# A new order of loads at the start of an attention and maxout kernel

## The chip, the cores and the metric

The kernel runs on one core of a Trainium2 chip. The core has TensorE (PE, matrix products into the accumulators called PSUM), VectorE (DVE), ScalarE (ACT), GpSimd (POOL) and SyncE (SP, which here only issues transfers), and sixteen DMA engines that all queues share. The metric is the device time of one execution in microseconds: the median of three runs.

## The reference, cut to what matters

Attention with a soft cap over 8 batches of 12 heads, 448 positions of 64 numbers, followed by a layer that takes the larger of two products:

```python
# q, k, v: (8, 12, 448, 64) f32, cap = 30
scores = cap * tanh((q @ k^T) / sqrt(64) / cap)
attn = exp(scores - max(scores)); attn = attn / (sum(attn) + 1e-9)
x = (attn @ v), heads side by side: (3584, 768)

h1 = x @ w1            # w1, w2: (768, 1024)
h2 = x @ w2
g = maximum(h1, h2)
out = g @ w_out        # w_out: (1024, 768), out: (3584, 768) f32
```

The kernel uses max(h1, h2) = h2 + relu(h1 - h2), so that

```
out = relu(x @ (w1 - w2)) @ w_out + x @ (w2 @ w_out)
```

It therefore prepares two matrices of its own: `wd_sb` = w1 - w2 (subtractions) and `wm_sb` = w2 @ w_out (transpositions of w2 and products on TensorE). After that each batch costs three products, with `wd_sb`, `wm_sb` and w_out.

## The kernel before

Two heads make a pair, two pairs a quad; there are 48 pairs and 24 quads. Three pairs make a group, and q, k, v are loaded group by group as f32, then cast to bf16. Groups 0 and 1 are transposed on TensorE (`transposes(i)`, one pair each); groups 2 and up by a transfer that transposes (`cross(g)`). Quad 0 needs pairs 0 and 1 (group 0), quad 1 pairs 2 (group 0) and 3 (group 1), quad 2 pairs 4 and 5 (group 1), quad 3 pairs 6 and 7 (group 2).

The loads and the preparation of the two matrices:

```python
    def load_wo(f):            # two of the eight 128-row pieces of w_out, 0.79 MB, cast on the way
        nc.gpsimd.dma_start(
            out=wo_sb[:, f : f + 2, :], in_=moe_w_out[f * P : (f + 2) * P, :].rearrange("(c p) n -> p c n", p=P)
        )

    def load_w2(c):            # one of the six 128-row pieces of w2, 0.52 MB, cast on the way
        nc.gpsimd.dma_start(out=w2b[:, c, :], in_=x_rows(moe_w2, c))

    def load_w1(c):
        w1_in[c] = opool.tile([P, DF], f32, name="osb") if c < OB else w1x[:, (c - OB) * DF : (c - OB + 1) * DF]
        nc.sync.dma_start(out=w1_in[c], in_=x_rows(moe_w1, c))

    def subtract(c, eng=nc.vector):
        eng.tensor_sub(wd_sb[:, c, :], w1_in[c], w2b[:, c, :])

    def turn_w2(c):            # 8 transpositions on TensorE, then one copy
        ps = mm_psum.tile([P, 512], f32, name="mm").bitcast(bf16)
        for f in range(FC):
            nc.tensor.transpose(ps[:, f * P : (f + 1) * P], w2b[:, c, f * P : (f + 1) * P], ident)
            yield
        w2T[c] = stage.tile([P, FC * P], bf16, name="w2T", bufs=2)
        nc.vector.tensor_copy(w2T[c], ps)

    def premultiply(c):        # 2 x 8 products
        for half in range(2):
            # ... ps = w2T[c] @ wo_sb[half], one product per yield ...
            nc.vector.tensor_copy(wm_sb[:, c, hs], ps[:, : DM // 2])
```

`w2b` lies in the buffer that later holds `gT`, the relu of the first product, so the first relu has to wait until w2 has been used up.

Scores go in three steps of two products into PSUM, each followed by tanh on ScalarE; `ex` is the exponential. `s_psum` has two buffers, `v_psum` one, and `mm_psum` two:

```python
    def scores(t, p, last=None):
        tanh[t, p] = att.tile([P, 2 * NJ, S], bf16, name="tanh")
        for j in range(NJ if p < 2 else 1):
            s = two_banks(last if last and j == NJ - 1 else s_psum)
            # ... two products into s ...
            nc.scalar.activation(tanh[t, p][:, 2 * j : 2 * j + 2, :], s[:, :, :S], AF.Tanh, scale=scale / cap)
```

`total(t)` sums the exponentials of a quad, `values(t)` multiplies them with v, `normalize` divides. All other TensorE work waits in a queue, and `F(n)` takes n products or transpositions from it, between the steps of the attention:

```python
    def F(n):
        rate[1] += n * rate[0]
        while rate[1] >= 1 and fill_q:
            try:
                next(fill_q[0])
                rate[1] -= 1
            except StopIteration:
                fill_q.pop(0)
```

The order in front, before the change (each engine works in this order):

```python
    fill_const(nc.vector, 0)
    load(0, "k", 0, 1); load(0, "q", 0, 1); load(0, "k", 1, L); load(0, "q", 1, L)
    load(1, "k"); load(1, "q"); load(0, "v")
    # ... casts of group 0's first pair ...
    for c in range(2): load_w2(c)
    for f in range(0, FC, 2): load_wo(f)
    fill_const(nc.gpsimd, 1)
    # ... transposes(0..2), scores and ex of quad 0, turn_w2(0) ...
    cast(nc.gpsimd, 1, "k"); cast(nc.gpsimd, 1, "q")
    for c in range(2, KC): load_w2(c)
    cast(nc.gpsimd, 0, "v", halves=(1,))
    load(1, "v"); load(2, "k"); load(2, "q")
    for c in range(KC): load_w1(c)
    # ... turn_w2(1); quad 1 with premultiply_first(0..8) and transposes(3..5) between ...
    cross(2)
    load(3, "k"); load(3, "q"); load(2, "v")
    # ... the queue gets turn_w2(2..5) and premultiply(1..5) ...
    total(0); scores(2, 0); ex(2, 0)
    F(4)
    normalize(0, values(0))
    F(8)

    for t in range(1, NQ):
        if t > 1:
            F(24 if t == 2 else 0)
            if more: scores(t + 1, 0, v_psum)
            ex(t, 2)
            F(6)
        if t == 2:
            # casts of k, q of group 3, cross(3), subtract(4), subtract(5) on POOL
        # ... F(2) F(3) F(3) F(2) with the sums of the exponentials between, if t > 1 ...
        if more: scores(t + 1, 1, v_psum)
        # ... F(3) F(4) F(3) F(4) ...
        if t == 1:
            for c in range(4): subtract(c, nc.gpsimd)
        F(8)
        if more: scores(t + 1, 2); ex(t + 1, 1)
        total(t)
        normalize(t, values(t))
        if t % 3 == 2: fill_q.append(moe(t // 3))   # 48 + 84 or 112 products of one batch
        F(9)
    F(10 ** 9)
```

Of the kernel before, what the change touches and what calls it, by code (L numbers as in the profile page):

```python
# [10 lines left out]
def kernel(  # L11
# [11 lines left out]
    nc = tc.nc  # L23
# [9 lines left out]
    P = 128  # L33
# [75 lines left out]
    def raw_of(g, what):  # L109
        if (g, what) not in raw:  # L110
            if (g, what) == (1, "v"):
                raw["unused"] = raw_tile(what)
            raw[g, what] = raw_tile(what)
        t = raw[g, what]
        m = t[:, : 2 * L * NJ * D].rearrange("p (h c) -> p h c", c=NJ * D)
        l = t[:, 2 * L * NJ * D :].rearrange("p (h d) -> p h d", d=D)
        return t, m, l
# [28 lines left out]
    def cast(eng, g, what, n0=0, n1=L, halves=(0, 1)):  # L146
# [52 lines left out]
    w1_in = {}  # L199
    w2b = (  # L200
        xpool.tile([P, FC, 2 * S], bf16, name="gT", bufs=1)
        .rearrange("p f s -> p (f s)")[:, : KC * DF]
        .rearrange("p (c n) -> p c n", c=KC)
    )

# [9 lines left out]
    def load_w2(c):  # L215
        nc.gpsimd.dma_start(out=w2b[:, c, :], in_=x_rows(moe_w2, c))

    w1x = xpool.tile([P, NP, 2 * S], bf16, name="xT").rearrange("p c s -> p (c s)").bitcast(f32)

    def load_w1(c):  # L220
        w1_in[c] = opool.tile([P, DF], f32, name="osb") if c < OB else w1x[:, (c - OB) * DF : (c - OB + 1) * DF]
        nc.sync.dma_start(out=w1_in[c], in_=x_rows(moe_w1, c))

    def subtract(c, eng=nc.vector):
        eng.tensor_sub(wd_sb[:, c, :], w1_in[c], w2b[:, c, :])

    w2T = {}

    def turn_w2(c):
        ps = mm_psum.tile([P, 512], f32, name="mm").bitcast(bf16)  # L230
        for f in range(FC):
            nc.tensor.transpose(ps[:, f * P : (f + 1) * P], w2b[:, c, f * P : (f + 1) * P], ident)
            yield
        w2T[c] = stage.tile([P, FC * P], bf16, name="w2T", bufs=2)
        nc.vector.tensor_copy(w2T[c], ps)

    def premultiply(c):

        for half in range(2):
            hs = slice(half * (DM // 2), (half + 1) * (DM // 2))  # L240
            ps = mm_psum.tile([P, 512], f32, name="mm")
            for f in range(FC):
                nc.tensor.matmul(  # L243
                    ps[:, : DM // 2], w2T[c][:, f * P : (f + 1) * P], wo_sb[:, f, hs],
                    start=(f == 0), stop=(f == FC - 1),
                )
                yield
            nc.vector.tensor_copy(wm_sb[:, c, hs], ps[:, : DM // 2])

# [37 lines left out]

    def scores(t, p, last=None):

        tanh[t, p] = att.tile([P, 2 * NJ, S], bf16, name="tanh")  # L290
        for j in range(NJ if p < 2 else 1):
            s = two_banks(last if last and j == NJ - 1 else s_psum)
# [98 lines left out]
    def moe(b):  # L391
        if b % 2 == 0:
            gT[b // 2] = xpool.tile([P, FC, 2 * S], bf16, name="gT", bufs=1)
        g, x = gT[b // 2], xT[b // 2]
        cs = slice((b % 2) * S, (b % 2 + 1) * S)
        for f in range(FC):
            ps = mm_psum.tile([P, 512], f32, name="mm")
            for c in range(KC):
                nc.tensor.matmul(  # L399
                    ps[:, :S], wd_sb[:, c, f * P : (f + 1) * P], x[:, c, cs], start=(c == 0), stop=(c == KC - 1)  # L400
                )
                yield
            nc.vector.tensor_relu(g[:, f, cs], ps[:, :S])  # L403
        for t in range(3) if b % 2 == 0 else range(3, 7):
            osb = opool.tile([P, DF], f32, name="osb")[:, :DM]
            ts = slice(t * P, (t + 1) * P)
            for half in range(2):
# [5 lines left out]
                for f in range(FC):  # L413
                    nc.tensor.matmul(  # L414
                        ps[:, : DM // 2], g[:, f, ts], wo_sb[:, f, hs], start=False, stop=(f == FC - 1)
                    )
                    yield
# [54 lines left out]

    fill_const(nc.vector, 0)
    load(0, "k", 0, 1)
    load(0, "q", 0, 1)
    load(0, "k", 1, L)
    load(0, "q", 1, L)
    load(1, "k")
    load(1, "q")
    load(0, "v")  # L480
    cast(nc.vector, 0, "k", 0, 1)
    cast(nc.gpsimd, 0, "q", 0, 1)
    for c in range(2):
        load_w2(c)
    for f in range(0, FC, 2):
        load_wo(f)
    fill_const(nc.gpsimd, 1)
    transposes(0)
    cast(nc.vector, 0, "k", 1, L)
    cast(nc.vector, 0, "q", 1, L)  # L490
    scores(0, 0, v_psum)
    ex(0, 0)
    transposes(1)
    scores(0, 1, v_psum)
    ex(0, 1)
    transposes(2)
    for _ in turn_w2(0):
        pass
    scores(0, 2)
    ex(0, 2)  # L500
    cast(nc.gpsimd, 1, "k")
    cast(nc.gpsimd, 1, "q")
    for c in range(2, KC):
        load_w2(c)
    cast(nc.gpsimd, 0, "v", halves=(1,))
    load(1, "v")
    load(2, "k")
    load(2, "q")
    for c in range(KC):
        load_w1(c)  # L510

    first = {}
# [23 lines left out]

    for _ in turn_w2(1):
        pass
    scores(1, 0, v_psum)
    transposes(3)  # L540
    cast(nc.vector, 0, "v", halves=(0,))
    cast(nc.gpsimd, 1, "v")
    cast(nc.gpsimd, 2, "k")
    cast(nc.gpsimd, 2, "q")
    ex(1, 0)
    premultiply_first(0, 2)
    scores(1, 1)
    ex(1, 1)
    premultiply_first(2, 4)
    transposes(4)  # L550
    premultiply_first(4, 6)
    scores(1, 2)
    ex(1, 2)
    transposes(5)
    cross(2)
    load(3, "k")
    load(3, "q")
    load(2, "v")
    premultiply_first(6, 8)
    for c in range(1, KC):  # L560
        if c + 1 < KC:
            fill_q.append(turn_w2(c + 1))
        fill_q.append(premultiply(c))
    total(0)
    scores(2, 0)
    ex(2, 0)
    F(4)
    normalize(0, values(0))
    F(8)

    for t in range(1, NQ):
        i = 2 * t
        more = t + 1 < NQ
        if t > 1:
            F(24 if t == 2 else 0)
            if more:
                scores(t + 1, 0, v_psum)
            ex(t, 2)
            F(6)
        if t in crosses:  # L580
            cross(crosses[t])
        if t == 2:
            cast(nc.gpsimd, 3, "k")
            cast(nc.gpsimd, 3, "q")
            cross(3)
            for c in range(4, KC):
                subtract(c, nc.gpsimd)
        if t == 3:
            cast(nc.gpsimd, 3, "v")
        if t > 2:  # L590
            extra(i)
        if t > 1:
            F(2)
            add(t, 0, 0)
            F(3)
            add(t, 0, 1)
            F(3)
            add(t, 1, 0)
            F(2)
        if more:  # L600
            scores(t + 1, 1, v_psum)
            ex(t + 1, 0) if t > 1 else None
        F(3)
        add(t, 1, 1)
        F(4)
        if t == 2:
            cast(nc.gpsimd, 2, "v")
            load(3, "v")
        F(3)
        add(t, 0, 2)  # L610
        F(4)
        add(t, 1, 2)
        if t == 1:
            for c in range(4):
                subtract(c, nc.gpsimd)
        if t == 2:
            extra(4)
            extra(5)
        if t > 2:
            extra(i + 1)  # L620
# [47 lines left out]
```

## Time and profile before

| | |
|---|---|
| time, median of 3 runs | 347.79 us (347.23 to 348.45) |
| span of the profiled execution | 345.9 us |
| TensorE busy | 326.2 us (94%) |
| ScalarE busy | 277.2 us (80%) |
| VectorE busy | 227.4 us (66%) |
| GpSimd busy | 109.8 us (32%) |
| moved by DMA | 61.78 MB |
| group 1's k and q, issued by 3.7 us | cast from 10.8 and 15.2 us on |
| crossbar transpose of group 2 | issued at 38.2 us, used at 48.3 us |

A busy share is taken over the whole span, which has stages with different limits; the start is a stage of its own. The profile counts a transfer's bytes as written: the loads of w2 and w_out, which cast from f32 to bf16 on the way, read twice what it shows. "Software queue" is the queue of the transfers that GpSimd issues, "hardware queue" that of SyncE.

### The profile page before, as it was taken

The page shows a single profiled execution, that of the slowest core. Times are in us where ns is not written, and L with a number is a line of the kernel's source. Part 1 is how long each engine was busy: PE and PEld are TensorE (multiplying, and loading weights), DVE is VectorE, ACT ScalarE, POOL GpSimd, SP SyncE. Part 2 cuts the span into 40 slices and gives each one's busy share as a digit, 9 for nine tenths or more (in the row PEclk, how much of TensorE's full clock was granted, in tenths as well). Part 3 has the DMA queues.
Part 4 walks back from the last instruction along what each step waited for, and adds up shares of the span by engine and source line. Part 5 has one row for each costly group of instructions (what it writes and reads, how often), then busy time and mean ns, then how long its engine had stood idle before and what let it go on. Part 6 is the DMA issues. An engine that isn't in the chain of part 4 may idle for free.

```text
span 345.9 us, 6777 instructions
## 1 busy us (share of the span) xinstructions
PE 326.2 (94%) x2710; PEld 163.3 (47%) x2710; DVE 227.4 (66%) x410; ACT 277.2 (80%) x241; POOL 109.8 (32%) x172
## 2 busy tenths in 40 slices
PE   3669979999999999999999999999999999999996
PEld 1324545445544554455444454454445554555563
DVE  5324645886777767777687768767776777874421
ACT  3998939989999999899999999799989999900000
POOL 6653848542144134304413431341343040000000
PEclk9959999999999999999999999999999999999999
DMA  7999999997695969775985499839956921012032
GB/s 253 252 253 242 369 204 180 247 213 199 132 295 158 211 149 282 205 172 123 252 252 100 134 230 300 179 96 216 307 124 143 209 96 46 2 47 91 0 93 91
DMA packets 103200, 61.78 MB, mean 179 GB/s; under 512 B 62337, under 2 KB 98177, under 8 KB 103169
## 3 DMA queue, kind: packets, MB, share of 16 engines
q1 hardware_dynamic: 101216, 58.21, 65.1%
q0 software_dynamic: 1952, 3.15, 5.0%
q8 instruction: 21, 0.34, 0.4%
q14 instruction: 11, 0.08, 0.1%
HBM read 42.47 MB, written 11.01 MB: 155 GB/s over the span
## 4 chain that ended last, share of the span: by engine, by line
PE 80%; DMA 13%; DVE 5%; issue 1%; SPq 0%; DVEq 0%
PE mm L414 22%; PE mm L399 19%; PE mm L411 16%; DMA kr<-in_k_dram 9%; PE v L366 6%; PE s L303 6%; DMA qkT<-kqf 3%; PE v L303 2%; PE s L300 2%; PE v L372 2%; PE mm L243 2%; PE s L350 2%; DMA osb<-in_moe_w_dram 1%; DVE xT L387 1%; DVE gT L403 1%; DVE st L352 1%
## 5 line engine op out<-in xcount | busy, mean ns | idle before, releaser
L309 ACT ACTIVATE expo<-tanh 128x2688 bf16<-128x2688 bf16 (+1 forms) x72 | 140.3, 1950 | 0.8 <-PE v L366 0.6
L304 ACT ACTIVATE tanh<-s 128x896 bf16<-128x896 f32 x122 | 106.4, 914 | 24.3 <-PE s L303 20.2
L414 PE MATMUL mm<-wo_sb,gT 128*128 128x384 bf16 x448 | 85.8, 327 | 0.0
L399 PE MATMUL mm<-xT,wd_sb 128*128 128x448 bf16 x384 | 78.8, 353 | 1.9 <-DVE gT L403 1.4
L411 PE MATMUL mm<-wm_sb,xT 128*128 128x384 bf16 x336 | 66.0, 326 | 0.4 <-DVE gT L403 0.4
L414 PEld LDWEIGHTS <-gT 128*128 128x128 bf16 x448 | 42.3, 98 | 34.7 <-issue 8.5
L418 DVE COPY osb<-mm 128x384 f32<-128x384 f32 x56 | 31.1, 555 | 40.7 <-PE mm L414 40.3
L399 PEld LDWEIGHTS <-wd_sb 128*128 128x128 bf16 x384 | 35.8, 98 | 41.2 <-issue 11.0
L403 DVE TENSOR_SCALAR gT<-mm 128x448 bf16<-128x448 f32 x64 | 39.4, 622 | 17.7 <-PE mm L399 17.2
L628 POOL COPY mark<-inv 1x1 f32<-1x1 f32 x18 | 3.2, 177 | 141.0 <-DVE inv L356 125.7
L411 PEld LDWEIGHTS <-xT 128*128 128x128 bf16 x336 | 31.7, 98 | 25.9 <-issue 5.9
L304 ACT ACTIVATE tanh<-v 128x896 bf16<-128x896 f32 x46 | 42.5, 923 | 0.0
L366 PE MATMUL v<-expo,vp 128*32 128x448 bf16 x576 | 35.6, 353 | 0.0
L303 PE MATMUL s<-qkT 64*128 64x448 bf16 x196 | 29.1, 371 | 6.7 <-ACT tanh L304 3.1
L387 DVE TENSOR_TENSOR xT<-v,inv 128x448 bf16<-128x448 f32 x48 | 27.8, 620 | 4.4 <-PE v L372 2.0
L352 DVE STREAM_TRANSPOSE st<-s 128x448 f32<-128x448 f32 x24 | 15.6, 650 | 19.8 <-PE s L350 17.5
L329 DVE TENSOR_TENSOR esum<-expo 128x896 bf16<-128x896 bf16 x42 | 27.9, 665 | 0.0
L327 DVE TENSOR_TENSOR esum<-esum,expo 64x896 bf16<-64x896 bf16 x42 | 26.6, 633 | 1.3
L331 DVE TENSOR_TENSOR esum<-esum,expo 128x896 bf16<-128x896 bf16 x42 | 26.7, 637 | 1.0
L303 PEld LDWEIGHTS <-qkT 64*128 64x128 bf16 x288 | 10.6, 96 | 29.7 <-issue 21.3
L366 PEld LDWEIGHTS <-vp 128*32 128x32 bf16 x576 | 15.3, 97 | 10.0
L183 POOL CAST kqf<-kr 128x1152 bf16<-128x1152 f32 x14 | 15.9, 1137 | 10.5 <-DMA kr<-in_k_dram 10.3
(66 smaller groups left out, 257.1 us busy)
## 6 DMA issues: line engine op xcount, KB each, us to landing
kr<-in_k_dram SPq DMA_DIRECT2D x14, 576.0 KB, 7.2
qr<-in_q_dram SPq DMA_DIRECT2D x14, 576.0 KB, 7.0
vr<-in_v_dram SPq DMA_DIRECT2D x14, 576.0 KB, 4.9
out_dram<-osb SPq DMA_DIRECT2D x20, 384.0 KB, 3.5
out_dram<-osb SPq DMA_DIRECT2D x16, 192.0 KB, 3.3
osb<-in_moe_w_dram SPq DMA_DIRECT2D x4, 512.0 KB, 8.6
gT<-in_moe_w_dram POOLq DMA_DIRECT2D x6, 256.0 KB, 12.8
wo_sb<-in_moe_w_out_dram POOLq DMA_DIRECT2D x4, 384.0 KB, 16.0
```

The lines of the kernel that those rows point to most:

```text
L303: nc.tensor.matmul(s[:, m, :S], k0[r, j * P : (j + 1) * P], qTn[r, :])
L304: nc.scalar.activation(tanh[t, p][:, 2 * j : 2 * j + 2, :], s[:, :, :S], AF.Tanh, scale=scale / cap)
L309: nc.scalar.activation(expo[t, p], tanh[t, p][:, 0:n, :], AF.Exp, scale=float(cap))
L329: nc.vector.tensor_add(d, e_of(t, ab, 0), e_of(t, ab, 1))
L331: nc.vector.tensor_add(d, d, e_of(t, ab, 2))
L366: nc.tensor.matmul(ps[r, :S], vp[g % 2][:, 2 * n + h, j, u::2], e_of(t, ab, j)[:, h, :], start=(j == 0), stop=False,)
L387: nc.vector.tensor_mul(x_of(t, u), ps[:, u, :S], inv[t])
L399: nc.tensor.matmul(ps[:, :S], wd_sb[:, c, f * P : (f + 1) * P], x[:, c, cs], start=(c == 0), stop=(c == KC - 1))
L403: nc.vector.tensor_relu(g[:, f, cs], ps[:, :S])
L411: nc.tensor.matmul(ps[:, : DM // 2], x[:, c, ts], wm_sb[:, c, hs], start=(c == 0), stop=False)
L414: nc.tensor.matmul(ps[:, : DM // 2], g[:, f, ts], wo_sb[:, f, hs], start=False, stop=(f == FC - 1))
L418: nc.vector.tensor_copy(osb[:, hs], ps[:, : DM // 2])
```

## The change

The order of the loads in front changes. The first piece of w2 and all of w_out now come directly behind group 0's q and k. Group 1's q, k, v are held back: a transfer of a single element of w_out into group 1's k buffer is put into the software queue in the middle of w_out, and since the load of k writes the same place, it has to wait for it. All loads of SyncE behind it wait with it. Group 1 is loaded and cast pair by pair, with pieces of w2 between. The products w2 w_out of the first piece are made between the scores of quads 0 and 1, as the pieces of w_out come; the rest is taken from the queue from quad 1 on. w1 is loaded in two column halves behind the transpose of group 2, w2 and `gT` lie in two half buffers, and subtractions are made by halves, partly on VectorE. The purpose is that TensorE has products to make while it would wait in front, and that what it needs first is loaded first.

The core of the diff:

```diff
-            if (g, what) == (1, "v"):
-                raw["unused"] = raw_tile(what)
...
     def load_w2(c):
-        nc.gpsimd.dma_start(out=w2b[:, c, :], in_=x_rows(moe_w2, c))
+        for part in range(2):
+            nc.gpsimd.dma_start(out=w2b[part][:, c, :], in_=x_rows(moe_w2, c)[:, part * DH : (part + 1) * DH])
...
-    def load_w1(c):
+    def load_w1(c, part):
...
-    def scores(t, p, last=None):
+    def scores(t, p, last=None, js=None):
...
-    for _ in turn_w2(1):
+    def load_and_cast(g, n):
+        for what in ("k", "q"):
+            load(g, what, n, n + 1)
+        for what in ("k", "q"):
+            cast(nc.gpsimd, g, what, n, n + 1)
+
+    fill_q.append(turn_w2(1))
+    fill_q.append(premultiply(1, 0))
+    for c in range(2, KC):
+        fill_q.append(turn_w2(c))
+        fill_q.append(premultiply(c - 1, 1))
+        fill_q.append(premultiply(c, 0))
+    fill_q.append(premultiply(KC - 1, 1))
+
+    fill_const(nc.vector, 0)
+    fill_const(nc.gpsimd, 1)
+    for n0, n1 in ((0, 1), (1, L)):
+        for what in ("k", "q"):
+            load(0, what, n0, n1)
+    load_w2(0)
+    load_wo(0)
+    load_wo(2)
+    nc.gpsimd.dma_start(out=raw_of(1, "k")[0][:1, :1], in_=moe_w_out[:1, :1])
+    load_wo(4)
+    load_wo(6)
+    load_w2(1)
...
+    scores(0, 0, v_psum)
+    ex(0, 0)
+    transposes(1)
+    scores(0, 1, js=(0, 1))
+    transposes(2)
+    for _ in turn_w2(0):
         pass
+    premultiply_first(0, 2)
+    scores(0, 1, js=(2,))
+    ex(0, 1)
+    scores(0, 2)
+    ex(0, 2)
+    load_and_cast(1, 0)
+    load_w2(2)
+    load_and_cast(1, 1)
+    load_w2(3)
+    load(0, "v")
+    cast(nc.gpsimd, 0, "v", halves=(1,))
+    load_and_cast(1, 2)
+    for c in range(4, KC):
+        load_w2(c)
+    load(2, "k")
+    load(2, "q")
+    load(1, "v")
     cast(nc.gpsimd, 2, "k")
     cast(nc.gpsimd, 2, "q")
+    cast(nc.gpsimd, 1, "v", halves=(1,))
+    premultiply_first(2, 4)
+    scores(1, 0, js=(0,))
+    premultiply_first(4, 6)
+    scores(1, 0, js=(1,))
+    premultiply_first(6, 8)
+    scores(1, 0, js=(2,))
     ex(1, 0)
+    transposes(3)
+    F(8)
+    scores(1, 1, v_psum)
     ex(1, 1)
+    F(24)
     transposes(4)
     scores(1, 2)
     ex(1, 2)
     cross(2)
     load(3, "k")
     load(3, "q")
+    for c in range(KC):
+        load_w1(c, 0)
+    cast(nc.vector, 0, "v", halves=(0,))
     total(0)
+    normalize(0, values(0))
     scores(2, 0)
     ex(2, 0)
+    F(14)
+    transposes(5)
+    scores(2, 1, v_psum)
+    F(6)
+    cast(nc.vector, 1, "v", halves=(0,))
+    F(6)
+    scores(2, 2)
+    ex(2, 1)
+    total(1)
+    normalize(1, values(1))
+    F(9)
+
+    for t in range(2, NQ):
...                       # pass t == 2:
+            for c in range(KC):
+                load_w1(c, 1)
+            load(2, "v")
+            load(3, "v")
+            for part in range(2):
+                for c in range(4 - part):
+                    subtract(c, part, nc.gpsimd)
...
+            for c in range(4, KC):
+                subtract(c, 0, nc.vector)
...                       # pass t == 3:
+            for c in range(3, KC):
+                subtract(c, 1, nc.vector)
```

## The prediction

> **What bounds the kernel now.** I read first the page's busy shares and its forty slices, then the busy time by stage of the first 60 us, then what TensorE (PE) waited for, and last the timeline around 38 to 60 us. The page:
>
> ```profile
> PE 326.2 (94%) x2710; PEld 163.3 (47%) x2710; DVE 227.4 (66%) x410; ACT 277.2 (80%) x241; POOL 109.8 (32%) x172
> ...
> PE   3669979999999999999999999999999999999996
> ...
> ACT  3998939989999999899999999799989999900000
> ...
> PEclk9959999999999999999999999999999999999999
> ```
>
> PE is full from the seventh slice (about 52 us) to the end, and ScalarE (ACT) has nothing more to do in the last five. So everything after about 60 us is PE's work in one unbroken stream, and the end comes earlier only if that stream starts earlier or has less in it. The change takes no matrix multiplication away; it can win only where PE stands idle or runs at half clock, in the first 50 us. By stage (columns: window, length, busy of PE, PEld, DVE, ACT, POOL, granted clock, DMA share, GB/s):
>
> ```profile
> 5.00:10.00 5.00, 3.09 (x46) 1.50 (x42) 2.95 (x6) 3.09 (x4) 4.92 (x10) 1.00 1.04 343
> ...
> 15.00:20.00 5.00, 2.46 (x37) 1.15 (x35) 1.02 (x2) 4.97 (x5) 3.44 (x6) 0.73 1.11 268
> 20.00:25.00 5.00, 2.97 (x11) 0.92 (x11) 2.04 (x4) 4.97 (x6) 2.20 (x4) 0.50 1.13 249
> 25.00:30.00 5.00, 5.00 (x76) 2.73 (x77) 1.41 (x3) 4.74 (x5) 2.82 (x6) 0.75 1.12 229
> ...
> 45.00:50.00 5.00, 3.62 (x26) 1.87 (x26) 1.09 (x2) 1.22 (x2) 1.63 (x1) 1.00 0.99 245
> ```
>
> All sixteen DMA engines are full (share about 1) from 5 us on; PE idles 2.5 and 2.0 us in the windows from 15 and 20 us; from 10 to 30 us ACT is the full one. Over the same ten stages to 50 us PE is busy 36.2 us, so 13.8 are idle. Who ended PE's idle time in the first 110 us:
>
> ```profile
> PE mm L273 <- DVE kqf L176: 3.9, 1, 3.9
> PE s L303 <- ACT tanh L304: 3.1, 2, 2.2
> ...
> PE s L303 <- DMA qkT<-kqf: 1.4, 1, 1.4
> ```
>
> The 3.9 us are the first load and stay. The third line is the crossbar transpose of group 2, which quad 3's first scores need:
>
> ```profile
> 38.16 8.01 SPq L279 DMA_TRANSPOSE qkT<-kqf  x1
> ...
> 48.31 0.55 PE L303 MATMUL s<-qkT 64*128 64x448 bf16 x4 [1.38 <-DMA qkT<-kqf]
> ```
>
> ACT lost 5.9 us to the same wait. It was issued at 38.16 and landed at 48.3: all six w1 pieces (3.1 MB) had been issued ahead of it.
>
> **What the Trainium skill says.** (1) "DMA: Bandwidth & Descriptors", section "Queues, rings and completion order": each engine goes round robin between queues, packet by packet. The trace agrees: from 15 to 20 us the software queue (GpSimd's casting loads) wrote 0.60 MB, read as 1.20 MB of f32, beside 0.72 MB of SyncE's queue. Together 1.92 MB in 5 us, or 0.38 MB per us. (2) "HBM Reference", section "Specifications": a core streaming alone passes the 358 GB/s per-core share, near 425. These 380 GB/s of reads lie between, so I take 0.38 MB/us as the supply when both queues are full. (3) "TensorE: Matmul & The Clock Gate", part 1: the clock halves after an idle window of about 3.4 us and comes back after as long a busy one. The 0.50 from 20 to 25 us, with PE busy 2.97 of 5, agrees; multiplications of 384 columns in this stretch took up to 528 ns against 326 later.
>
> **The change, part by part.** In what follows a "fill" is one multiplication or transposition that F takes from the queue.
>
> *Loads.* To cross group 2, quad 3 needs k, q of groups 0 to 2 (4.1 MB), v of group 0 (0.7), w2 and w_out (6.3) in both kernels: 11.1 MB, or 29 us at 0.38. Moving w1 behind the transpose takes 3.1 MB, about 8 us of supply, from ahead of it. This is the main gain I see for the transpose. The hold costs no supply if the software queue is full meanwhile; it has 4.2 MB issued by about 9 us.
>
> *The hold.* The software loads are issued from about 3.2 us on (two microseconds of zeroing now come first). In the trace before, the first of them was issued at 4.64 us and hardly moved before 8.8, so I start them at 7 us. At 0.37 MB/us w2's first part (0.52 MB) has landed at 10, w_out's first quarter (0.79) at 12, its second at 14; the one element comes with it. Group 1's first pair is then issued at 14.4 and, with a third of the supply beside the rest of w_out, lands at about 21. Two casts on POOL (1.4 us), the transposes on PE and their copy (1.8) make it ready at 24. ACT by then has finished quad 0 at 18.5 as before, three tanh of quad 1 (0.9 each) and an exponential (2.44): 23.6 at best, 24.3 with the wait for w_out's last quarter (19.2, then four multiplications). So the hold is nearly hidden: about 0.8 us later than ACT's 23.5 before.
>
> *PE from 24 to 45 us.* scores(1,1), then 24 fills, which need w2's part 2, landing at about 27.5 since POOL issues it only after the casts. With fills at half clock the group ends at 30 to 31.5, against 29.5 for ACT's work on quad 1; so ACT idles about 1.7 us. From there PE does scores(1,2) 0.5, total and values 2.5, scores(2,0) 0.8, 14 fills 1.7, transposes and copy 1.5, scores(2,1) 0.8, 12 fills 1.8, then follows ACT's tanh to scores(2,2), total and values 3.2, and 9 fills 1.5. That puts scores(3,0) at 45.2 to 46.5, against 48.31. The transpose of group 2 is issued at about 36.7 after POOL's casts, with only v of group 1 and the last w2 beside it, and takes about 6.8 us: 43.5. It is off the path.
>
> *Quad 3's pass to the next one.* From 48.31 to 59.95 (scores(4,0)) before, 11.6 us with ACT nearly full. The new stretch has the same scores, sums and fills, so scores(4,0) comes at 56.8 to 58.1: 3.1 to 1.8 us earlier.
>
> *What is owed.* By that point the kernel before has taken 114 fills: 112 of w2 w_out and two of the first MoE product. The new one has put w2's second transposition into the queue too: 120, and its slots (67 before the loop, 47 in pass 2) give 114. It is behind by six of 0.167 us (22 took 3.68 in the chain) and two of 0.189 (48 took 9.08), 1.4 us, paid at the end.
>
> *w1 in halves.* Left halves come after k, q of group 3, landing near 51, and are subtracted by 55; the first MoE product needs them at about 58. Right halves come behind group 3's transpose (issued about 50, 4.3 us of SyncE), landing near 61.5. VectorE's three subtractions of right halves stand in its order at about 62, the fifth product at 64. Likely no wait, little margin.
>
> Sum: 3.1 to 1.8 earlier, less 1.4, gives 0.4 to 1.7 us. I add about a microsecond for stretches where PE, now better fed from 24 us on, warms its clock sooner than I assumed: half clock cost some 4 us of work between 16 and 28 us. So about 2.3 us below 347.8: **345.5 us**.
>
> **Rivals.** *A: the hold starves ACT.* If the software queue alone runs below 0.37 MB/us, or starts late again, group 1 comes 3 us later, ACT waits near 24 us, and every later step shifts. For it: software loads took 12.4 to 19.1 us to land for w_out before. Against: they shared the engines then, and had 0.81 of the 1.14 MB written in the window from 25 to 30 us. It makes 348 to 350. *B: w1's right halves come late.* VectorE then stands in a subtraction, PSUM isn't emptied, PE stops. For it: SyncE is held by each transpose (8.0 us in the profile shown). Against: these waits fall after some w1 traffic has drained. It makes 346.5 to 349. *C: PE fills the gaps.* If nearly all idle time after the first load but the ACT waits goes, and with it the half clock, the gain is up to 7 us: 340 to 342. For it: 9.9 us idle after the first load. Against: ACT, full from 10 to 30 us, sets the pace of scores there, and the same multiplications are still behind loads.
>
> **Range and chances.** Mine and a mix of C draw down, A and B up; 341.5 to 349.0 should hold it. More than 2% faster means below 340.8, all of C: 0.10. More than 2% slower, above 354.7, needs a wait of 8 us that I don't see: 0.03. Within 2%: 0.87.
>
> **What would show it.** Right: group 1's first k landing near 20 us; the wait on the crossbar transpose gone before scores(3,0), which starts at 45 to 46.5; the next scores(4,0) at 57 to 58; PE full thereafter. Wrong: a wait of PE or ACT on group 1's casts of over 2 us near 22 us (A); VectorE idle before a subtraction and PE waiting for PSUM at 60 to 66 us (B); PE's idle time before 50 us below 8 us with clock 1.00 (C). The prediction falls if PE loses its full stream after 60 us, as my sum leaves everything there as it was.

## The result, and the profile after

The changed kernel takes 351.85 us (median; 349.80 to 352.79), the kernel before, beside it, 347.99 us (347.23 to 348.45). The ratio is 1.0105 with a 95% interval of 1.0069 to 1.0141: about 1% slower, within 2%. The prediction was 345.5 us, with a range of 341.5 to 349.0; the time lies above the range, and the sign was wrong.

The page of the changed kernel, with the rows that were shown for the one before:

```profile
span 347.9 us, 6814 instructions
...
PE 325.1 (93%) x2710; PEld 162.6 (47%) x2710; DVE 234.8 (67%) x419; ACT 277.2 (80%) x241; POOL 110.3 (32%) x184
...
PE   3777799699999999999999999999999999999995
...
ACT  3698999689998999899989999799989999800000
...
PEclk9999999999999999999999999999999999999999
```

The span is 2.0 us longer than before (345.9), though PE is busy 1.1 us less and the granted clock reads 1.00 throughout: this profile is of one of the quickest executions of the changed kernel. Slices two, three and six show PE fuller, as intended; four and five, where some work was done at half clock before, are emptier; and the eighth (about 61 to 70 us), a 9 before, is a 6. The busy time by stage says the same (columns as before: PE, PEld, DVE, ACT, POOL, clock, DMA share, GB/s):

```profile
15.00:20.00 5.00, 4.56 (x17) 1.49 (x16) 0.00 (x0) 3.55 (x3) 0.48 (x2) 1.00 1.13 286
20.00:25.00 5.00, 3.36 (x50) 1.86 (x50) 2.28 (x4) 4.94 (x6) 4.71 (x13) 1.00 1.08 367
25.00:30.00 5.00, 3.31 (x25) 1.78 (x24) 1.25 (x2) 4.97 (x5) 4.77 (x11) 1.00 1.18 241
...
45.00:50.00 5.00, 5.00 (x45) 2.46 (x37) 3.33 (x6) 4.32 (x5) 3.31 (x4) 1.00 1.05 324
60.00:65.00 5.00, 3.94 (x24) 1.66 (x23) 4.97 (x9) 4.97 (x7) 1.33 (x2) 1.00 1.09 275
65.00:70.00 5.00, 3.42 (x23) 1.48 (x25) 4.22 (x6) 2.00 (x2) 3.49 (x6) 1.00 1.14 263
```

From 15 to 20 us PE has 4.56 us of work where it had 2.46 (part of it slow work: four products with w_out take 1.48 us at 17.03 and four of the same shape 0.82 at 18.74, although the granted clock reads 1.00 at both), and from 45 to 50 us it is full. In its place idle time has come from 25 to 30 us (it was full there) and from 60 to 70 us: PE is busy 7.36 of these ten, against 9.81 before. VectorE is full from 60 to 65 us. What PE waited for in the first 110 us (total, times, longest):

```profile
PE mm L278 <- DVE kqf L174: 4.4, 2, 4.0
PE mm L405 <- DVE gT L411: 2.6, 3, 1.4
PE s L309 <- ACT tanh L310: 2.6, 3, 1.1
...
PE mm L238 <- DMA gT<-in_moe_w_dram: 1.7, 2, 1.0
```

The first line is the first load, as before. The wait for the crossbar transpose is gone. Two lines have grown: the first MoE product (L405) waits for VectorE's relu, which empties PSUM (0.2 us before), and w2's transpositions (L238, whose tile carries the name of the buffer that w2 shares with `gT`) wait for a load (0.4 us before).

A yardstick for all runs is the time of the third scores of each quad, in order on PE. "Pass 3 to 4" is the stretch from quad 3's to quad 4's; in it the first MoE product begins.

| us | quad 1 | quad 3 | quad 4 | pass 3 to 4 | quad 23 | end |
|---|---|---|---|---|---|---|
| before | 27.98 | 55.47 | 68.94 | 13.47 | 298.30 | 345.9 |
| after, profile of the result (clock 1.00) | 30.72 | 53.12 | 69.16 | 16.04 | 298.96 | 347.9 |
| after, profile of the repeat below (clock 0.995) | 32.73 | 55.37 | 71.41 | 16.04 | 301.21 | 350.1 |

One part of the story is the pass: 2.6 us longer in both executions. The second is the front, where the two differ by 2 us. The third is what comes behind quad 4: from there to the end both take 278.7 us, against 276.9 before.

### The profile page after: what moved, and what is told of

Read it like the earlier page. It is cut to its first block, busy times and chain, and to the rows that moved or that the text cites. A ratio compares the mean times of both kernels' runs of the same rounds, so it can differ in the third digit from the quotient of the medians.

```text
span 347.9 us, 6814 instructions
## 1 busy us (share of the span) xinstructions
PE 325.1 (93%) x2710; PEld 162.6 (47%) x2710; DVE 234.8 (67%) x419; ACT 277.2 (80%) x241; POOL 110.3 (32%) x184
## 4 chain that ended last, share of the span: by engine, by line
PE 83%; DVE 7%; DMA 6%; POOL 2%; issue 1%; ACT 0%; DVEq 0%; POOLq 0%
PE mm L422 22%; PE mm L405 18%; PE mm L419 16%; PE v L372 7%; PE s L309 6%; PE mm L248 4%; PE v L378 2%; PE s L306 2%; DMA kr<-in_moe_w_out_dram 2%; PE v L309 2%; DMA gT<-in_moe_w_dram 2%; PE s L356 2%; DMA kr<-in_k_dram 2%; DVE gT L411 2%; DVE esum L333 1%; DVE xT L393 1%
## 5 line engine op out<-in xcount | busy, mean ns | idle before, releaser
L405 PE MATMUL mm<-xT,wd_sb 128*128 128x448 bf16 x384 | 78.8, 353 | 4.1 <-DVE gT L411 4.1
L405 PEld LDWEIGHTS <-wd_sb 128*128 128x128 bf16 x384 | 35.8, 98 | 43.3 <-issue 12.6
L310 ACT ACTIVATE tanh<-v 128x896 bf16<-128x896 f32 x45 | 41.6, 925 | 0.0
L393 DVE TENSOR_TENSOR xT<-v,inv 128x448 bf16<-128x448 f32 x48 | 27.8, 620 | 2.5
L337 DVE TENSOR_TENSOR esum<-esum,expo 128x896 bf16<-128x896 bf16 x42 | 28.0, 668 | 0.9
```

The costliest lines, as they stand in the source:

```text
L337: nc.vector.tensor_add(d, d, e_of(t, ab, 2))
L393: nc.vector.tensor_mul(x_of(t, u), ps[:, u, :S], inv[t])
L405: nc.tensor.matmul(ps[:, :S], wd_sb[:, c, f * P : (f + 1) * P], x[:, c, cs], start=(c == 0), stop=(c == KC - 1))
```

## The experiments

Two theories share the loss between them. The VectorE theory: VectorE is too full in the pass from quad 3 to 4, from its share of the w1 subtractions, and PE waits for PSUM. The front theory: PE waits for w2's third piece and loses its clock, which costs what the transpose gains. The rivals: the hold itself, ACT's wait in front, or the right halves of w1 coming late by DMA. In the expectations V is the VectorE theory, C the front theory (not rival C of the prediction), H the hold, and L that w1 had to make way for the transpose. The ratios are to the kernel before, with 95% intervals.

### The changed kernel again (e0_again)

No edit.

> The changed kernel once more, unaltered. Its profiled execution took 349.8 us with the granted clock at 1.00 throughout, while its other three took 351.7 to 352.8 with 0.990 to 0.995. If a half-clock stretch in front is worth about 2 us (theory C), executions with a mean clock of 0.99 to 0.995 again lie about 2 us above those with 1.00, and the profile shows where the stretch lies: before 30 us, with TensorE then late at quad 3's scores by about 2 us. If the spread is something else, times don't go with the clock.

Measured: 352.35 us, 1.0102 (1.0072 to 1.0131). Of ten executions, two had a mean clock of 0.998 or more and took 349.8; six of 0.993 to 0.997 took 352.3; two of 0.990 took 352.7 (medians). The kernel before shows no such split between its two usual clocks: over all runs below its median is 348.35 us both at 0.985 or less (86 executions) and at 0.998 or more (26); three at 0.994 took 350.3 to 350.8. The two executions part at the wait for w2's third piece. The profile of the result, PE's timeline (start, length, instruction, idle time before it and what ended it):

```profile
27.43 0.40 PE L238 MATMUL mm<-ident,gT 128*128 128x128 bf16 x4 [1.02 <-DMA gT<-in_moe_w_dram]
...
28.73 1.46 PE L248 MATMUL mm<-wo_sb,w2T 128*128 128x384 bf16 x8
```

and of the repeat, the same view:

```profile
28.16 0.40 PE L238 MATMUL mm<-ident,gT 128*128 128x128 bf16 x4 [1.68 <-DMA gT<-in_moe_w_dram]
...
29.48 2.40 PE L248 MATMUL mm<-wo_sb,w2T 128*128 128x384 bf16 x8
```

with its busy time by stage:

```profile
30.00:35.00 5.00, 4.41 (x51) 1.95 (x49) 2.36 (x4) 2.86 (x3) 4.70 (x8) 0.67 1.11 258
```

The wait is 0.66 us longer, and then the same eight multiplications take 2.40 us instead of 1.46: the clock was halved, 0.67 on the mean of this window. Quad 1 is 2.0 us later and quad 3 2.25, and nothing is caught up: the repeat ends 2.2 us later. So in this execution, and by their mean clocks in most, half clock comes back in front, and eats all that the transpose gains: scores(3,0) start at 48.49, against 48.31 before. The Trainium skill, "TensorE: Matmul & The Clock Gate", part 1, says that the activity window runs free of the kernel, so that the same kernel meets it at another phase each time; two executions that part in this way agree with it, though no run here shows the window itself, and here the wait is longer too. Runs e5 and e13 below part with waits of the same length.

### VectorE's subtractions to POOL (e1_sub_pool)

```diff
-                for c in range(4 - part):
+                for c in range(4 + 2 * part):
                     subtract(c, part, nc.gpsimd)
...
-        if t == 3:
-            for c in range(3, KC):
-                subtract(c, 1, nc.vector)
```

> The last three subtractions of w1's right halves are made on POOL, behind its others, instead of on VectorE in the middle of quad 4's pass. Theory V (VectorE's backlog in that pass cost the gain): from quad 3's third scores to quad 4's takes 13.5 to 14 us instead of 16.0, and the whole is 2 to 2.5 us faster than the changed kernel, so 0.99 to 1.005 of the kernel before. Theory H (the hold made ScalarE late in front and this is never made up): no change, 1.01. POOL may be late with v of group 2 by 1 us at most, as it stood idle for 4 us before that cast.

Measured: 351.73 us, 1.0090 (1.0067 to 1.0113); the pass takes 15.45 instead of 16.04. VectorE's timeline:

```profile
63.09 1.37 DVE L335 TENSOR_TENSOR esum<-expo 128x896 bf16<-128x896 bf16 x1
64.50 1.46 DVE L337 TENSOR_TENSOR esum<-esum,expo 128x896 bf16<-128x896 bf16 x1
```

A sum of exponentials, 0.61 us alone, takes 1.37 and 1.46 while POOL subtracts (two in 2.66 us from 62.83) and casts. VectorE is rid of 1.9 us of subtractions, and the quad's six sums grow from 4.98 to 6.18 us together (4.38 in the kernel before). The Trainium skill, "SBUF — State Buffer", section "Who interferes with whom", says that a VectorE instruction with two inputs in SBUF and a GpSimd instruction that reads SBUF exclude each other from a shared port. The trace agrees: the relu of the same pass, whose input lies in PSUM, stays at 0.61. So the work moved, and 1.2 of the 1.9 us came back.

### Without the one-element transfer (e2_no_hold)

```diff
-    nc.gpsimd.dma_start(out=raw_of(1, "k")[0][:1, :1], in_=moe_w_out[:1, :1])
```

> The one-element transfer is left out, all else as in the changed kernel. Theory H: group 1 comes by 14 us, ScalarE is 2 us earlier from quad 1 on and the whole 1 to 2 us faster. Theory V: w_out shares the engines with group 1, the products of w2's first piece, which stand ahead of the third scores of quad 0, wait for it, ScalarE stops 3 to 5 us near 14 us; the whole is the same as the changed kernel or up to 3 us slower (1.01 to 1.02 of before).

Measured: 353.43 us, 1.0144 (1.0117 to 1.0170): no faster, by the medians 1.1 us slower than the repeat. PE's waits:

```profile
PE v L490 <- DMA wo_sb<-in_moe_w_out_dram: 3.8, 4, 1.3
```

Without the hold group 1 shares the engines with w_out, and PE, whose order puts w_out's products between quad 0 and quad 1, waits for it; the products in between are still slow (four in 1.44 us at 23.86). The wait for w2's third piece is gone here, so the hold does cost that wait, but leaving it out costs more. The hold isn't the loss.

### Quad 0's scores ahead of the first products (e3_scores_first)

```diff
-    scores(0, 1, js=(0, 1))
+    scores(0, 1)
+    ex(0, 1)
     transposes(2)
+    scores(0, 2)
+    ex(0, 2)
     for _ in turn_w2(0):
         pass
     premultiply_first(0, 2)
-    scores(0, 1, js=(2,))
-    ex(0, 1)
-    scores(0, 2)
-    ex(0, 2)
```

> All scores of quad 0 are put ahead of the transposition of w2 and the first four products; loads and hold as in the changed kernel. ScalarE's wait of 2.84 us at 16.4 us goes. Theory H: the whole gains 2 to 3 us. Theory V: ScalarE then waits for group 1 or for w2's third piece instead (it lands at 27 to 28 us in any case), quad 3's scores stay within 1 us of 46.5, and the whole gains less than 1 us.

Measured: 352.66 us, 1.0122 (1.0096 to 1.0148). In the changed kernel ACT waits 2.84 us, to 16.42, since these scores stand behind w_out's first products. Here quad 0's third scores come at 14.04 instead of 16.39, and quad 1's at 32.50 instead of 32.73: what ACT gains, it waits for again (1.45 us at 19.91 and 3.16 at 33.49), and PE's wait for w2's third piece, ahead of quad 1's third scores, grows to 3.3 us. Taking ACT's wait away gained nothing.

### The right halves of w1 earlier (e4_w1_right_early)

```diff
-    for c in range(KC):
-        load_w1(c, 0)
+    for part in range(2):
+        for c in range(KC):
+            load_w1(c, part)
...    # and load_w1(c, 1) is taken out of pass t == 2
...    # VectorE's subtract(3..5, 1): from t == 3 to the end of pass t == 2
```

> w1's right halves are loaded directly behind the left ones, ahead of group 3's transpose, in a stretch where SyncE waits for casts; so VectorE's three right subtractions are made at the end of quad 3's pass, and group 2's v, group 3's v come earlier, so their casts too. Theory V in its second form (VectorE's queue in quad 4's pass is full of its own subtractions, 2.0 us, and of sums drawn out by POOL's work on SBUF at the same time, 1.3 us, which is why handing the subtractions to POOL gained only 0.6): quad 3's third scores to quad 4's takes 13.5 to 14.2 us instead of 16.0, and the whole is about 2 us faster than the changed kernel, 1.003 to 1.006 of before. If something else holds that pass (products waiting for the relu's buffer, the transfers), it stays above 15.5 us.

Measured: 353.56 us, 1.0153 (1.0119 to 1.0187). The halves have landed early and the subtractions are still dear. VectorE's timeline:

```profile
54.29 2.45 DVE L231 TENSOR_TENSOR wd_sb<-xT,gT 128x512 bf16<-128x512 f32 x2
56.66 1.65 DVE L231 TENSOR_TENSOR wd_sb<-osb,gT 128x512 bf16<-128x512 f32 x1
```

One takes 0.68 us alone, these three 0.89, 1.64 and 1.65, as POOL subtracts without a break from 49.0 to 57.8. The pass takes 17.62, with a wait of PE of 1.8 us for VectorE's division (L393). In the changed kernel a late arrival of w1 isn't the cause.

### w2's third piece early (e5_w2_early)

```diff
     load_w2(1)
+    load_w2(2)
...
     load_and_cast(1, 0)
-    load_w2(2)
-    load_and_cast(1, 1)
     load_w2(3)
+    load_and_cast(1, 1)
```

> w2's third piece is issued directly behind the second, not behind the casts of group 1's first pair. Theory C (TensorE's wait of about 2.4 us for that piece at 27 to 29 us, and the half clock it brings, cost about 4 us of quad 1): the wait goes, the half-clock stretch near 30 us goes or becomes rare, quad 1's third scores come at 28.5 to 30.5 us instead of 32.7, and the whole is 1.5 to 2.5 us faster than the changed kernel (1.003 to 1.006). If the loads were the limit, group 1 comes 1.4 us later for it, ScalarE waits there instead, and nothing is gained.

Measured: 351.24 us, 1.0086 (1.0060 to 1.0112). The wait for w2 is gone, the clock full, and quad 1 comes at 28.98, quad 3 at 52.58: 2.8 us earlier than in the repeat. But quad 4 comes at 70.80, only 0.6 earlier: the pass takes 18.2 us, and PE's wait for the relu grows from 2.6 to 4.2 us. The front theory holds for the front, and the pass takes nearly all of it back: w1 doesn't come earlier when the front does, POOL waits 2.92 us for its right halves, and its subtractions (58.54 to 62.30) fall beside VectorE's first two sums, which take 1.44 and 1.46 us. Besides, a new wait of 2.1 us has come in front, on VectorE's cast of v, which lies beside POOL's casts.

### Both, and both with fewer fills owed (e6_both, e7_both_debt)

e6 is e4 and e5 together. e7 adds:

```diff
-    F(24)
+    F(8)
     transposes(4)
+    F(16)
...
-    F(14)
     transposes(5)
+    F(22)
```

> Both of these together. If the two costs are independent, the gains add: 4 us faster than the changed kernel, within 1 us of before (0.997 to 1.002). What is then left of the loss is the debt of eight fills (1.4 us), set against the earlier transpose.

> Both, and the debt paid in front: eight more fills (14 to 22) ahead of the second scores of quad 2, with the transposes of pairs 4 and 5 set ahead of fills so that their copies are hidden. The eight fills take 1.4 us; about 2 us of TensorE's idle time between 35 and 41 us are there for them. If they fit, 1 to 1.4 us faster than the kernel with both alone, 0.992 to 0.998 of before; if ScalarE sets the pace there, they only push its tanh back and nothing is gained.

Measured: 353.84 us, 1.0150 (1.0125 to 1.0176), and 352.45 us, 1.0110 (1.0081 to 1.0140). In e6 PE waits 5.6 us for VectorE's copy of a w2 w_out product: it stands behind VectorE's subtractions, which are drawn out and themselves wait 2.08 and 1.06 us for w1 to land. With a front this early w1 does come late. Quad 3 comes at 50.63, earlier than in any other run, and quad 4 at 73.34, later than in any other: the pass takes 22.7 us. Eight fills more before scores(2,1), and the transposes earlier (e7), bring the median down by 1.4 us, to that of the repeat and no lower. In its profile (of its quickest execution, 350.2) quad 4 comes at 70.95, and from there to the end it takes 277.3 us, against 278.7 in the changed kernel: the eight fills are worth the 1.4 us predicted.

### VectorE's three subtractions left out (e8_no_dve_sub)

This kernel leaves three of the twelve half subtractions out: those columns of `wd_sb` are zeroed early and stay zero, so its output isn't the reference's. The products are the same in number.

```diff
     ex(0, 0)
+    nc.vector.memset(wd_sb[:, 3:, DF // 2 :], 0.0)
...
-        if t == 3:
-            for c in range(3, KC):
-                subtract(c, 1, nc.vector)
```

> The changed kernel without VectorE's three subtractions of right halves (those columns of w1 - w2 are set to zero early instead, so the output isn't the reference's). Theory V: 2.0 us of VectorE's work goes, and the sums drawn out by POOL's casts (1.3 us) stay; quad 4's pass takes 14 us instead of 16.0 and the whole is about 2 us faster than the changed kernel (1.003 to 1.006 of before). If that pass is held by something else, it stays at 15.5 us or more and so does the time.

Measured: 349.76 us, 1.0042 (1.0024 to 1.0061): by the medians 2.6 us less than the repeat, by the ratios 2.1. The pass takes 14.25, so the three subtractions account for 1.8 of the 2.57 us. The six sums, beside POOL's casts of v, still take 4.67 us.

### w1 whole, ahead of the transpose, and all subtractions on POOL (e9_w1_front)

```diff
+    for part in range(2):
+        for c in range(KC):
+            load_w1(c, part)
     cast(nc.gpsimd, 2, "k")
...
     cast(nc.vector, 0, "v", halves=(0,))
+    for part in range(2):
+        for c in range(KC):
+            subtract(c, part, nc.gpsimd)
...    # all other load_w1 and subtract taken out; w2's third piece early as in e5
```

> w1 is loaded whole ahead of group 2's transpose, as in the kernel before, and POOL makes all twelve half subtractions by about 50 us, before VectorE's sums begin with quad 3; w2's third piece early; everything else (hold, order of products, halves) as changed. Theory V: VectorE's sums in quad 4's pass take 0.6 us each, the pass takes 13.5 us, the transpose of group 2 lands at 45 to 47 us and costs TensorE at most 1 us, and the whole is 1.5 to 3.5 us faster than the changed kernel, 0.995 to 1.004 of before. Theory L (w1 had to get out of the transpose's way): TensorE waits 2 us or more for the transpose, or for group 3's, and the time is that of the changed kernel.

Measured: 352.40 us, 1.0123 (1.0105 to 1.0142). The pass is short, 14.26, but quad 3 only at 57.12. In front VectorE's cast of v takes 3.00 us for two instructions (1.10 in the changed kernel) beside POOL's work, PE waits 2.4 us for it, and half clock follows from 34 to 40 us (0.51 on the mean). That this is the same port isn't shown.

### The old kernel with the other's parts (e10_before_f32, e15_before_f32_sub)

In e10, eight more fills ahead of scores(3,0), where the kernel before waits for its transpose; in e15, all six subtractions also go to POOL at t == 1.

```diff
-            F(24 if t == 2 else 0)
+            F(32 if t == 2 else 0)
...    # e15 only
-            for c in range(4, KC):
-                subtract(c, nc.gpsimd)
...
-            for c in range(4):
+            for c in range(KC):
                 subtract(c, nc.gpsimd)
```

> The kernel before with one number changed: 32 fills instead of 24 ahead of quad 3's first scores. TensorE stands idle there for 1.4 us until the transpose of group 2 lands, and eight products take 1.3 us. If the end is set by how much TensorE has done by then (the ledger of idle time and debt), the whole gets 1.0 to 1.4 us faster, 0.996 to 0.998 of before, with quad 3's scores within 0.3 us of where they were. If quad 3's scores or VectorE's copies are put back by as much, it stays the same.

> The kernel before with 32 fills instead of 24 ahead of quad 3's scores, as tried, and with all six subtractions made by POOL in one go before the casts of group 3. There, in the one tried, TensorE waited 1.4 us for a subtraction that POOL made only after those casts. If that wait was what ate the gain, this is 1 to 1.4 us faster than before (0.996 to 0.998); if the later start of group 3's casts puts back the scores that need them, or the transpose again lands later, no gain.

Measured: 349.22 us, 1.0020 (1.0001 to 1.0039), and 348.27 us, 1.0004 (0.9993 to 1.0015). The wait for the transpose stays, 1.4 and 1.6 us: it landed later (49.4 in e10). In e10 PE then waits 1.4 us for POOL's last subtraction. Neither edit gains anything in the old order.

### Without the three subtractions, and w2's third piece early (e11_no_dve_sub_w2)

e5 and e8 together; it leaves out the same three subtractions as e8.

> The changed kernel with both costs taken out: VectorE's three subtractions left out (so the output isn't the reference's) and w2's third piece issued early. If the two are independent, 1.1 us (what the early piece alone gained) comes on top of the 2.6 us of leaving the subtractions out: 0.999 to 1.003 of before, so that without its two new waits the new order of loads gains nothing over the old. If the pass of quad 4 is held by the arrival of w1's right halves and POOL's work on them rather than by VectorE's own subtractions, an earlier front is lost again in that pass: it takes over 15.5 us and the time stays at 1.004.

Measured: 347.96 us, 0.9992 (0.9973 to 1.0011). Quad 3 comes at 52.11, 3.4 us before the old kernel's 55.47, but the pass still takes 15.29: PE waits 1.2 us for VectorE's division, which stands behind two subtractions that wait 1.40 us for w1's left halves and take 2.44 us beside POOL's. So quad 4 comes at 67.40, 1.5 us before the old kernel's 68.94, and the end at 346.1, against 345.9: what is owed has eaten the rest.

### Quad 3's sums on TensorE (e12_ns4, e13_w2_early_ns4, e14_before_ns4)

In all kernels the sums of exponentials go over to VectorE from quad 3 on. With the constant at 4, quad 3's six sums are made by 16 products on TensorE instead; everything else stays, the subtractions and the arrival of w1 too. e12 is the changed kernel with this, e13 also has w2's third piece early, e14 is the kernel before with it.

```diff
-    NS = 3
+    NS = 4
```

> The changed kernel with one number changed: the sums of exponentials of quad 3 are made by TensorE (16 products) as for quads 0 to 2, not by VectorE, so that VectorE's queue in quad 4's pass loses six operations of 0.6 us and more (3.7 us, with their drawn-out part 5), and TensorE gains 12 products (0.75 us). Output as the reference's. Theory V: that pass takes 14.2 to 14.8 us instead of 16.0 and the whole is 1.2 to 2 us faster than the changed kernel (1.004 to 1.008 of before). If w1's right halves themselves come too late, the pass keeps 15.5 us or more and nothing is gained.

> The same with w2's third piece issued early. Alone, the early piece brought quad 3's third scores forward by 2.8 us but the pass after them grew to 18.2 us. Theory V: without quad 3's sums on VectorE the pass takes 14.5 to 15.5 us, and the whole is 0.995 to 1.001 of before. If the pass is held by the arrival of the right halves, quad 4's third scores stay at 70.5 us and the time at 1.007.

> The kernel before with the sums of quad 3 made by TensorE, as a control. VectorE isn't the bound of quad 4's pass there, so by both theories it pays 12 products, 0.75 us, and may win a little from shorter waits for the relu: 1.000 to 1.003 of before. If it gets over 1 us faster, VectorE bounded that pass in the kernel before too.

Measured: 349.32 us, 1.0028 (1.0011 to 1.0044); 348.72 us, 1.0011 (0.9996 to 1.0026); 348.61 us, 1.0004 (0.9990 to 1.0018). The pass takes 13.14, 13.13 and 13.14 us; the 16 products come behind quad 4's third scores, where they cost 0.6 us (e12 and e14 take that much longer from quad 4 to quad 23). PE's waits in e12 from 55 to 110 us:

```profile
PE mm L419 <- DVE gT L411: 0.6, 1, 0.6
```

and VectorE's timeline:

```profile
63.88 1.28 DVE L231 TENSOR_TENSOR wd_sb<-xT,gT 128x512 bf16<-128x512 f32 x2
65.08 1.27 DVE L411 TENSOR_SCALAR gT<-mm 128x448 bf16<-128x448 f32 x2
```

The subtractions keep their place in VectorE's order and take what they took, and the waits at L405 are gone: it is VectorE's load in this pass, not the subtraction as such. With the same edit in both, the pass of the changed kernel is as long as that of the old one (13.14 in e12 and e14), and the old kernel's time gains nothing: the 2.57 us that the pass had lost are VectorE's. (The medians give back 3.0 us and the ratios 2.6, but 11 of e12's 22 executions had a clock of 0.998 or more, against two of ten of the changed kernel; among those e12 is 1.4 us quicker, among those of 0.993 to 0.997 2.7.)

e13 has the wait on VectorE's cast of v that e5 has. PE's timeline in e5, then in e13:

```profile
32.51 0.75 PE L372 MATMUL v<-expo,vp 128*32 128x448 bf16 x12 [2.12 <-DVE vp L154]
```

```profile
32.68 0.75 PE L372 MATMUL v<-expo,vp 128*32 128x448 bf16 x12 [2.12 <-DVE vp L154]
```

The waits are equally long. In e5 the clock stays full and the next eight products with w_out take 1.47 us; in e13 it is halved (0.50 from 34 to 38 us) and they take 2.74. So the length of the wait alone doesn't decide.

## Why the prediction was wrong

**The transpose.** Right in the profile of the result, where scores(3,0) start at 46.50 and scores(4,0) at 57.54, within "45.2 to 46.5" and "56.8 to 58.1". SyncE's timeline, and PE's:

```profile
34.00 4.18 SPq L284 DMA_TRANSPOSE qkT<-kqf  x1
```

```profile
46.50 0.55 PE L309 MATMUL s<-qkT 64*128 64x448 bf16 x4
...
57.54 0.55 PE L309 MATMUL s<-qkT 64*128 64x448 bf16 x4
```

It was issued 2.7 us earlier than I said and landed at 39.9, after 5.9 us (I had 6.8). In the repeat, and by their mean clock in most executions, half clock takes these 2 us away (48.49 and 59.79).

**The hold.** Right. Group 1's first k landed at 19.4 us, ACT is full from 20 to 30 us (4.94 and 4.97 of 5), and without the hold the kernel is no faster (e2). Rival A falls. The landings that I gave for w2's first part and w_out's first two quarters (10, 12 and 14) came out, at 9.7, 11.9 and 13.7, but with some luck: 0.37 MB/us from 7 us on gives 8.4, 10.5 and 12.7.

**What is owed.** Right in kind. From quad 23's third scores to the end it takes 48.94 us in the profile of the result, 47.6 before, and another 0.4 goes between quads 4 and 23: 1.8 us in all. The eight fills made in front in e7 take 1.4 off this, as predicted; the other 0.4 is not explained.

**"w1 in halves ... Likely no wait, little margin."** This is the step that failed. What rival B foretold, a PE that stops because PSUM isn't emptied, is what happened, though not for B's reason: I looked at when the right halves land, and not at what else VectorE has to do then. VectorE's timeline in the profile of the result:

```profile
62.14 0.69 DVE L231 TENSOR_TENSOR wd_sb<-osb,gT 128x512 bf16<-128x512 f32 x1
62.74 1.29 DVE L231 TENSOR_TENSOR wd_sb<-xT,gT 128x512 bf16<-128x512 f32 x2
63.94 0.62 DVE L411 TENSOR_SCALAR gT<-mm 128x448 bf16<-128x448 f32 x1
64.48 1.03 DVE L337 TENSOR_TENSOR esum<-esum,expo 128x896 bf16<-128x896 bf16 x1
65.43 0.61 DVE L411 TENSOR_SCALAR gT<-mm 128x448 bf16<-128x448 f32 x1
65.97 2.11 DVE L333 TENSOR_TENSOR esum<-esum,expo 64x896 bf16<-64x896 bf16 x2
```

and what it makes PE wait for:

```profile
64.61 1.29 PE L405 MATMUL mm<-xT,wd_sb 128*128 128x448 bf16 x6 [1.06 <-DVE gT L411]
66.10 1.29 PE L405 MATMUL mm<-xT,wd_sb 128*128 128x448 bf16 x6 [0.19 <-DVE gT L411]
68.78 0.54 PE L405 MATMUL mm<-xT,wd_sb 128*128 128x448 bf16 x2 [1.39 <-DVE gT L411]
```

VectorE stands in no subtraction: none has idle time before it, so w1 was there (its last right half landed at 60.5). They are simply 1.9 us more of work in a row, and the sums behind them are drawn out beside POOL's casts of v from 63.67 on (L337 1.03 instead of 0.62). A relu that PE needs comes behind all of it. PE's three waits are 2.64 us, the pass is 2.57 longer. In the kernel before, four of the six subtractions were done by POOL at 38 to 47 us, before VectorE has any sums, and two at 56 to 61, mostly ahead of the sums:

```profile
38.22 8.40 POOL L225 TENSOR_TENSOR wd_sb<-osb,gT 128x1024 bf16<-128x1024 f32 x4
...
56.53 4.22 POOL L225 TENSOR_TENSOR wd_sb<-xT,gT 128x1024 bf16<-128x1024 f32 x2
```

Leaving the three out shortens the pass by 1.8 us (e8), and taking the sums away instead brings it to what the old kernel has with the same edit (e12, e14), with the loads of w1 issued as before; earlier arrival (e4) and another engine (e1) don't help, since POOL and VectorE then get in each other's way. "The prediction falls if PE loses its full stream after 60 us" is what came true.

**The microsecond for the clock.** "I add about a microsecond for stretches where PE ... warms its clock sooner": wrong in most executions. I had w2's third piece land at 27.5, which is right for its first half (PE goes on at 27.43, for the second at 28.50), but counted no cost from the wait beyond its length; in the repeat the clock was halved after 2.4 us of waits between 26.5 and 29.3 us, and quad 1 came 2 us later. Point (3) of the prediction, half clock after an idle window of about 3.4 us, I called confirmed too soon. Measured, less is enough: the longest wait just before half clock is 1.68 us in the repeat and 2.12 in e13. The pieces of w2 are issued behind POOL's casts, which wait for the held load: here is where the hold does cost.

**The sum.** Predicted 3.1 to 1.8 us, less 1.4, plus 1. In the profile of the result: 2.35 us earlier at quad 3, 2.57 lost in the pass, 1.8 behind quad 4, so 2.0 later at the end. Without the failed step 0.5 us would be left of the gain, inside the 0.4 to 1.7 that I had before adding the microsecond. In the repeat: 0.1 us earlier at quad 3 (the transposes' gain, less the half clock), 2.57 lost in the pass, then the same 1.8: 4.3 us, which is the distance from the profile of before (350.1 and 345.9) but for rounding. In e11 the front keeps 3.4 us; 1.8 go in the pass and 1.8 behind it, and nothing is left (0.9992).

**Rival C** falls as well: gaps in PE that are filled open elsewhere. Up to 50 us PE is idle 14.0 us in the profile of the result, where C wanted less than 8, and 13.8 in the kernel before; up to 60 us it is 14.5 in the repeat and 14.0 before.

What stays open: what decides whether a wait is followed by half clock, the phase of the clock's window or something else, and so the share of executions that lose the 2 us, was not controlled; and I found no version that beats the kernel before. An order that owes nothing at the end, with all these waits away, was not tried. Nor was the front of e11 had together with the pass of e12: e13, meant for that, met half clock and had quad 3 at 55.07. From e11's quad 3 (52.11), e12's pass (13.14) and its 279.3 us behind it the end would come at 344.6 us by my estimate, against 345.9.

## What to carry to other kernels

When work is moved between engines, add up all that the receiving engine has to do in that stretch, not only whether the data come in time: VectorE, busy 7.87 of the ten microseconds from 60 to 70 before, had no room for 1.9 more in a row, ahead of a relu that was waited for. Work on GpSimd isn't free for VectorE: here VectorE's operations with two inputs in SBUF took up to twice their time and more beside GpSimd's work (a sum 1.46 us for 0.61, a subtraction 1.65 for 0.68), GpSimd's subtractions up to 1.61 for 1.16, so moving a subtraction between them brought only part of it back. And before filling a gap in front, ask who pays for the work pushed back: here eight fills not taken in front cost 1.4 us behind.

## What was unexpected in the hardware

Waits of TensorE of 1.68 and 0.69 us within 3 us were followed by half clock, waits of 1.02 and 0.67 us were not: two executions that part by 0.7 us of waiting end 2.2 us apart. One and the same wait of 2.12 us was followed by half clock in e13 and not in e5. And VectorE's cast of v, which has one input in SBUF, was also drawn out beside GpSimd, 3.00 us for two against 1.10; yet in the profile of the result GpSimd casts at the same time and the two take 1.10, so which of its instructions does it stays open.
